# Attention steps in another order: both pairs' scores together, the quarters last

## The chip, the cores and the metric

The kernel runs on one core of one Trainium2 chip. The metric is device time in microseconds (us) of one execution; what is compared is the median of several. One execution of the kernel before was also recorded by the hardware profiler, and all traces shown are of that one.

The engines are named as the profile names them: PE is TensorE's products and PEld its loading of weights, DVE is VectorE, ACT is ScalarE, POOL is GpSimd, SP is SyncE, which issues every DMA of this kernel. Granted clock is the share of TensorE's full clock that the chip allowed.

## The reference

Sigmoid attention over 8 batches of 12 heads, 448 tokens, 64 numbers a head, then a dense layer with a squared ReLU:

```python
scores = scale * np.matmul(q, k.transpose(0, 1, 3, 2)) - np.log(S)
attn = 1.0 / (1.0 + np.exp(-scores))
attn_out = np.matmul(attn, v)
x = attn_out.transpose(0, 2, 1, 3).reshape(B * S, H * D)   # 3584 x 768
h = x @ w_in                                               # w_in is 768 x 2048
g = s * np.maximum(h, 0) ** 2 + b
out = g @ w_out                                            # 2048 x 768
```

All inputs of attention are float32; the two weight matrices arrive as float64 and are handed to the chip as pairs of words.

## The kernel before, in words

**Stages.** First attention, head by head, with its result written to DRAM as tokens (`x_dram`). Then, for the first 512 tokens, a plain dense layer (`ffn1`, `ffn2`) over 16 blocks of the hidden width. During this the weights are split in a rounded part and a rest and combined in sums, which are stored to DRAM (`wd`). Last, for two groups of three times 512 tokens, a fast scheme with fewer products reads these sums back as tiles `wu`; its first half writes `h`, its second half `o`.

**A quad.** Attention goes through 24 quads: four heads of one batch, as two pairs. The two heads of a pair lie on the two halves of the 128 partitions. For each pair `scores` makes three tiles `psc` of 128 keys by 448 queries, both heads side by side; a sigmoid on ScalarE (L347) turns each into a tile `a` in SBUF. The 448 keys are three blocks of 128 and a rest of 64. The rests of all four heads share one tile, `psc_l`, whose products use quarters of the array (`scores_last`, L368). `attn_v` (L378) multiplies `a` with v into `pav`, 64 columns a head, and `attn_v_last` (L387) adds the quarters. A product in float32 goes through TensorE in two passes, so each of these instructions stands twice in the profile. The score tiles rotate through three PSUM buffers, `pav0` and `pav1` have one each.

**A step.** The loop is pipelined over quads: step n makes the scores of quad n's first pair, attn @ v of both pairs of quad n-1, the scores of quad n's second pair and its quarters, and then the quarters of attn @ v of quad n-1. The result is copied from PSUM (`store_x`: the first pair by VectorE, the second by ScalarE) and stored.

**Weights beside attention.** A piece is a block of 128 rows or columns of one weight matrix: 768 float64 per partition, 768 KB. `piece` fetches it into a tile `st` and turns it into float32 with five VectorE instructions (L192 takes out the exponent; L198, L201, L205, L208) and one of ScalarE (L196) behind the first. All 32 pieces are done during attention, by a list that says how many belong to each step (`PIECES`). `sums_out` makes the sums of w_out and stores them. Which job comes in which part of a step is set by hand, with `at_step(n, when, fn)`; `ticks` runs the jobs of a part in the order of `when`.

**What sets the order.** Every engine runs its instructions in the order in which the program issues them. All DMAs go through SP, and its queue uses eight semaphores in turn (`DMAHW0` to `DMAHW7` in the program's waits), so a DMA is issued only after the eighth before it has landed. Slots of SBUF are handed out by hand (`Slots`); a tile in a reused slot waits for the earlier tile's last use.

**At the start** TensorE multiplies zeros (`idle`, six times) while the first loads run.

**At the change to the fast scheme** `load_raw` loads tokens (tiles `a_mk`, 512 KB each), `fetch` the tiles `wu` six ahead of use, and `out_store` writes the first outputs.

Of the kernel before, what the change touches and what calls it, by code (L numbers as in the profile page):

```python
# [11 lines left out]
F32 = mybir.dt.float32  # L12
# [71 lines left out]
def sigmoid_attention_relu2_ffn(  # L84
# [55 lines left out]

    heap = Slots(pool(ctx, "h0", 1), 1, "g")
    first = ExitStack()
    cx = Slots(pool(first, "cx", 1), 7, "c")
# [10 lines left out]
    nc.vector.memset(nls, -math.log(S))  # L154
    nc.scalar.activation(e_bias, nls, AF.Sigmoid)
    nc.vector.memset(e_bias, -896.0 * 2.0**23)
# [7 lines left out]
    def f32(ap):  # L164
        return ap.bitcast(F32)
# [4 lines left out]
    def sub(o, x, y):  # L170
        nc.vector.tensor_tensor(o, x, y, op=ALU.subtract)
# [100 lines left out]
    def sums_d(l, p, tl):  # L272

        _, x, sign, y = SUMS[l][3]
        t = tl.tile([P, 2, 2, KW], F32R, name=f"td_{l}_{p}")
        for j in range(2):
            op(f32(t[:, j, 1]), block(l, 2 * p + j, x), sign, block(l, 2 * p + j, y))
        yield
        nc.scalar.copy(t[:, :, 0], f32(t[:, :, 1]))
        yield  # L280
        sub(t[:, :, 1], f32(t[:, :, 1]), f32(t[:, :, 0]))
        nc.sync.dma_start(wd[l][p][:, 9], f32(t).rearrange("p j h c -> p j (h c)"))
        tl.free(t)
        yield
# [31 lines left out]


    at = ExitStack()
    ap_ = pool(at, "ap", 10)
    xo = pool(at, "xo", 3)  # L320
    ldv = pool(at, "ldv", 3)
    qk = ExitStack()
# [69 lines left out]
    def store_x(b, t, pavs):  # L392
        for i in range(2):
            o = xo.tile([P, S], F32, tag="xo", name=f"xo_{b}_{t}_{i}")
            if i:
                nc.scalar.copy(o, pavs[i][:, :S])
            else:
                nc.vector.tensor_copy(o, pavs[i][:, :S])  # L398
            nc.sync.dma_start(x_dram[b][:, 2 * t + i], o)

    loaded = {0: load(*quads[0], first=True)}

    zero = xo.tile([P, S], F32, tag="xo", name="zero").bitcast(BF16)
    nc.vector.memset(zero, 0.0)
    idle = ps_qk.tile([P, 2, 512], F32, tag="psc", name="idle")
    for _ in range(WARM):
        nc.tensor.matmul(idle[:, 0, :S], zero[:, :P], zero[:, :S], start=True, stop=True)

    plan = {}
    stores = []

    def at_step(n, when, fn):
        plan.setdefault((n, when > 5), []).append((when, len(plan.get((n, when > 5), ())), fn))

    def piece(l, f, n):
        st = []

        def fetch():
            st.append(cx.tile([P, DM], I64, name=f"st_{l}_{f}"))
            nc.sync.dma_start(st[0], (w_in, w_out)[l][f])

        at_step(n - 2, 5, fetch)
        g = []

        def last():
            next(g[0])
            cx.free(st[0])  # L430

        at_step(n - 1, 6, lambda: (g.append(convert(l, f, st[0])), next(g[0])))
        at_step(n - 1, 7, lambda: next(g[0]))
        at_step(n, 1, lambda: next(g[0]))
        at_step(n, 1, last)

    def sums_out(f, n):
        g = []
        at_step(n - 1, 8, lambda: (g.append(sums(1, f, cx)), next(g[0])))
        at_step(n, 2, lambda: next(g[0]))  # L440
        at_step(n, 9, lambda: next(g[0]))
        at_step(n + 1, 2, lambda: next(g[0]))
        at_step(n + 1, 9, lambda: next(g[0]))
        if f % 2:
            d = []
            at_step(n, 8, lambda: (d.append(sums_d(1, f // 2, heap)), next(d[0])))
            at_step(n + 1, 2, lambda: next(d[0]))
            at_step(n + 1, 9, lambda: next(d[0]))

    pieces = iter([(l, f + h * NP) for f in range(NP) for l in (1, 0) for h in range(2)])  # L450
    for n, m in enumerate(PIECES):
        for _ in range(m):
            piece(*next(pieces), n)
# [1 line left out]
    for f in range(NP):  # L455
        sums_out(f, SUMS_AT[f])

    def ticks(n, end=False):
        for _, _, fn in sorted(plan.pop((n, end), ()), key=lambda x: x[:2]):
            fn()  # L460

    loaded[1] = load(*quads[1])
    nc.sync.dma_start(s_sb, s)
    nc.sync.dma_start(b_sb, b_)
    ticks(-1)

    x0 = []
    blk = ExitStack()
# [14 lines left out]
        cx.free(w)  # L483
        return ph

    def first_tokens():
        for h in range(2):
            lo = cx.tile([P, HC, TB], F32R, name=f"x0l_{h}")
            load_tokens(f32(lo), 0, HC * h, HC)
            x0.append(lo)  # L490
        for h in range(2):
            yield
            lo = x0[h]
            hi = cx.tile([P, HC, TB], F32R, name=f"x0h_{h}")
            nc.scalar.copy(hi, f32(lo))
            sub(lo, f32(lo), f32(hi))
            x0[h] = (hi, lo)
        yield

    prev = None  # L500
    for n in range(NL + 1):
        cur = quads[n] if n < NL else None
        a, pavs = [], []
        if cur:
            a.append(scores(*cur, 0, loaded[n]))
        ticks(n)
        if n == NL - 2:
            ft = first_tokens()
            next(ft)
        if prev:  # L510
            for i in range(2):
                pavs.append(attn_v(*quads[n - 1], i, loaded[n - 1], prev[i]))
        if cur:
            a.append(scores(*cur, 1, loaded[n]))
            a.append(scores_last(*cur, loaded[n]))
        if prev:
            attn_v_last(loaded[n - 1], prev[2], pavs)
# [5 lines left out]
        if prev:  # L523
            store_x(*quads[n - 1], pavs)
        ticks(n, True)
        if n == NL - 1:
            qk.close()
            ps_h = pool(blk_ps, "ps_h", 2, space=PSUM)
            ps_av = pool(at, "ps_av2", 1, space=PSUM)
            next(ft)  # L530
            w1 = base(0, 0)
            next(ft)
        prev = a
    ph0 = ffn1(order[0], w1)
    at.close()

# [2 lines left out]
    p2 = pool(blk, "p2", 3)  # L539
    gp = pool(blk, "gp", 3)  # L540
    ps_o = pool(blk_ps, "ps_o", 1, space=PSUM)
    cx.more(pool(blk, "t2", 1), 5, "t")
    assert not plan

    threes = [tuple(1 + 3 * n + i for i in range(3)) for n in range((NT - 1) // 3)]
# [128 lines left out]
    for i, f in enumerate(order):  # L674
        ph = ffn1(f, w1) if i else ph0
        if i + 1 < NF:
            w1 = base(0, order[i + 1])
        if i == 0:
            w2[0] = base(1, order[0])
        for k in (k for k in range(NP) if 0 < i - sums_at[k] < 3):  # L680
            next(ts[k])
            next(ts[k])
        next(td, None)
        if i in sums_d_at:
            td = sums_d(0, sums_d_at.index(i), cx)
            next(td)
        if i and i in sums_at:
            next(ts[sums_at.index(i)])
        g = activate(f, ph)
        if i + 1 < NF:  # L690
            w2[i + 1] = base(1, order[i + 1])
        if i == 0:
            next(ts[0])
        if held:
            ffn2(*held, i == 1, False)
        held = (w2[i], g)
        if i == NF - 4:
            load_raw(0, *start[0])
            early.close()
            roll = pool(ctx, "roll", ROLL, side="right")  # L700
            heap.more(pool(ctx, "h1", 1, side="right"), 14, "r")
            for m, k in start[1:3]:
                load_raw(0, m, k)
            for _ in range(4):
                fetch()
        if i == NF - 3:
            for m, k in start[3:6]:
                load_raw(0, m, k)
            fetch()
        if i == NF - 2:  # L710
            for _ in range(5, AHEAD):
                fetch()
            for m, k in start[6:]:
                load_raw(0, m, k)
    for q_ in (4, 3):
        for fn in todo.pop(q_):
            fn()
# [17 lines left out]
    for o in outs:  # L735
        heap.free(o)
    ps = pool(ctx, "ps", 4, space=PSUM)

    def act_square(x):
# [24 lines left out]
    for n, blocks in enumerate(threes):  # L764
# [316 lines left out]
```

## Time and profile before

| | |
|---|---|
| time, median of 3 runs | 1069.99 us (1069.43 to 1070.44) |
| time of the profiled execution | 1071.2 us |
| its span, first to last instruction | 1069.4 us |
| mean granted clock | 0.998 |
| attention, to its last quarter | 0 to 277.65 us |
| plain dense layer | 277.65 to about 408 us |
| fast scheme | about 408 us to the end |
| HBM traffic | 262 GB/s over the span |

A row of a timeline gives start, length, engine, line, operation, what it writes and reads, the number of instructions merged in it, and in brackets how long the engine had stood idle before and what ended that. Rows of the chain that ended last give start, length and what the time went to. Groups give count, busy time, mean length in ns and idle time before them with its causes. A row of windows gives the stretch, its length, busy time of PE, PEld, DVE, ACT and POOL with the instructions touched, the granted clock, and the DMA engines' busy share and GB/s.

### The profile page before, as it was taken

Reading aid. Unit: us, or ns where it says so; the run is one execution under the profiler, and the core shown is the slowest. Engines: PE = TensorE matmul, PEld = TensorE weight load, DVE = VectorE, ACT = ScalarE, POOL = GpSimd, SP = SyncE. Lnnn points to the kernel's source line nnn. Section 1 sums busy time; section 2 is a strip of 40 time slices with the busy share of each in tenths; the row PEclk is TensorE's granted clock in tenths of the full one; section 3 lists DMA queues with packets and bytes.
Section 4 is the critical chain, followed back from the end, with each engine's and each line's share of the span. In section 5 each row is a group of like instructions: output and inputs, shape, how many; then the busy total and the mean of one; then the engine's idle time right before and its main releaser. Section 6 shows DMA issues by size and latency. Waiting matters only on the chain.

```text
span 1069.4 us, 13380 instructions
## 1 busy us (share of the span) xinstructions
PE 1059.4 (99%) x4998; PEld 753.7 (70%) x4998; DVE 780.7 (73%) x889; ACT 593.5 (55%) x662; POOL 0.2 (0%) x4
## 2 busy tenths in 40 slices
PE   8999999999999999999999999999999999999998
PEld 3333333333688887888888888888888888888886
DVE  3767766788787866365788889698545788888776
ACT  6878778778776656345336453343445336443432
POOL 0000000000000000000000000000000000000000
PEclk9999999999999999999999999999999999999999
DMA  7899888999898999766666677897666666676673
GB/s 288 274 351 361 315 319 331 364 334 335 310 394 321 371 359 405 234 194 196 196 192 189 194 233 227 263 325 270 197 194 196 195 190 191 194 230 220 213 229 109
DMA packets 105328, 280.86 MB, mean 263 GB/s; under 512 B 10544, under 2 KB 26416, under 8 KB 105264
## 3 DMA queue, kind: packets, MB, share of 16 engines
q1 hardware_dynamic: 105264, 280.01, 77.4%
q8 instruction: 40, 0.66, 0.2%
q14 instruction: 24, 0.20, 0.1%
HBM read 195.04 MB, written 84.93 MB: 262 GB/s over the span
## 4 chain that ended last, share of the span: by engine, by line
PE 94%; DMA 5%; ACT 0%; SPq 0%; DVE 0%; issue 0%; DVEq 0%; ACTq 0%
PE o L1024 31%; PE h L902 29%; PE psc L356 10%; PE pav L378 10%; PE ph L478 5%; PE po L659 5%; PE psc_l L368 2%; PE pav L387 2%; DMA wd<-w 1%; DMA st<-w_out 1%; DMA wu<-wd 1%; DMA a<-xd 1%; DMA wd<-t 1%; DMA q<-q_t 0%; SPq L311 0%
## 5 line engine op out<-in xcount | busy, mean ns | idle before, releaser
L347 ACT ACTIVATE a<-psc,nls 128x896 f32<-128x896 f32 x144 | 134.1, 1002 | 48.8 <-PE psc L356 48.7
L902 PE MATMUL h<-s_0h,wu 128*128 128x512 f32 x480 | 149.2, 392 | 1.8 <-DMA wu<-wd 1.8
L902 PE MATMUL h<-s_1h,wu 128*128 128x512 f32 x480 | 148.0, 389 | 0.0
L356 PE MATMUL psc<-q,k 64*128 64x448 f32 x576 | 122.8, 559 | 0.8 <-ACT a L347 0.8
L378 PE MATMUL pav<-a,v 128*64 128x448 f32 x576 | 113.5, 543 | 0.0
L902 PEld LDWEIGHTS h<-s_0h,wu 128*128 128x128 f32 x480 | 90.8, 189 | 21.1 <-ACT G L780 2.2
L902 PEld LDWEIGHTS h<-s_1h,wu 128*128 128x128 f32 x480 | 90.1, 188 | 18.8
L780 ACT COPY G<-h 128x1024 f32<-128x1024 f32 x48 | 48.8, 1017 | 96.8 <-PE h L902 68.1
L356 PEld LDWEIGHTS psc<-q,k 64*128 64x128 f32 x576 | 51.9, 188 | 71.0 <-issue 43.8
L747 ACT ACTIVATE G<-G,b_sb,s_sb 128x1024 f32<-128x1024 f32 x48 | 59.8, 1246 | 62.9 <-DVE G L744 62.2
L168 DVE TENSOR_TENSOR G<-G,h 128x1024 f32<-128x1024 f32 x40 | 48.8, 1219 | 62.2 <-PE h L902 62.2
L902 PE MATMUL h<-s_0l,wu 128*128 128x512 f32 x240 | 94.0, 391 | 0.0
L902 PE MATMUL h<-s_1l,wu 128*128 128x512 f32 x240 | 93.4, 389 | 0.0
L378 PEld LDWEIGHTS pav<-a,v 128*64 128x64 f32 x576 | 39.2, 137 | 71.4 <-issue 62.4
L1024 PE MATMUL o<-g_0h,wu 128*128 128x512 f32 x240 | 78.8, 389 | 0.0
L1024 PE MATMUL o<-g_1h,wu 128*128 128x512 f32 x240 | 78.8, 389 | 0.0
L1024 PE MATMUL o<-g_2h,wu 128*128 128x512 f32 x240 | 78.8, 389 | 0.0
L1024 PE MATMUL o<-g_3h,wu 128*128 128x512 f32 x240 | 78.8, 389 | 0.0
L659 PE MATMUL po<-g,w 128*128 128x512 f32 x288 | 67.7, 389 | 0.0
L659 PEld LDWEIGHTS po<-g,w 128*128 128x128 f32 x288 | 54.1, 188 | 11.2
L478 PE MATMUL ph<-x0h,w 128*128 128x512 f32 x192 | 61.7, 390 | 0.0
L398 DVE COPY xo<-pav 128x448 f32<-128x448 f32 x24 | 15.0, 624 | 60.5 <-PE pav L387 40.6
(127 smaller groups left out, 1831.2 us busy)
## 6 DMA issues: line engine op xcount, KB each, us to landing
wu<-wd SPq DMA_DIRECT2D x240, 512.0 KB, 3.5
wd<-t SPq DMA_DIRECT2D x48, 768.0 KB, 7.8
st<-w_out SPq DMA_DIRECT2D x16, 768.0 KB, 10.0
st<-w_in SPq DMA_DIRECT2D x16, 768.0 KB, 9.8
wd<-w SPq DMA_DIRECT2D x16, 768.0 KB, 4.3
v<-v_t SPq DMA_DIRECT2D x24, 448.0 KB, 7.2
xd<-xo SPq DMA_DIRECT2D x48, 224.0 KB, 8.8
k<-k_t SPq DMA_DIRECT2D x23, 448.0 KB, 4.5
```

What stands on the lines that cost most here:

```text
L168: nc.vector.tensor_tensor(o, x, y, op=ALU.add)
L347: nc.scalar.activation(a, psc[:, :, :S], AF.Sigmoid, bias=nls, scale=SCALE)
L356: nc.tensor.matmul(psc[:, j, :S], kt[r, i, c * P : (c + 1) * P], qt[r, i, :], start=True, stop=True,)
L368: nc.tensor.matmul(psc[half[i], j, :S], kt[r, i, 3 * P :], qt[r, i, :], start=True, stop=True,)
L378: nc.tensor.matmul(pav[r, :S], ld_[2][:, 3 * i + c, j, :], a[c][:, j, :], start=c == 0, stop=False,)
L387: nc.tensor.matmul(pavs[i][r, :S], ld_[2][half[i], 6, j, :], a[half[i], j, :], start=False, stop=True,)
L478: nc.tensor.matmul(ph, w[:, k, wi, kc * P : (kc + 1) * P], x0[h][xi][:, cc, :], start=m == 0, stop=m == 3 * NCC - 1,)
L659: nc.tensor.matmul(pos[e], w[:, k, wi, kc * P : (kc + 1) * P], g[:, gi, :], start=first and i == 0, stop=last and i == 2,)
L747: nc.scalar.activation(x, x, AF.Identity, bias=b_sb, scale=s_sb)
L780: nc.scalar.copy(g(m, h), bk)
L902: nc.tensor.matmul(bk[:, j], wt[:, j, wi, c * P : (c + 1) * P], opd[i][xi][:, c, :], start=i == ch[0] and m == 0, stop=m == 3 * KC - 1, sk ...
L1024: nc.tensor.matmul(bk[:, e], wt[:, f, wi, e * P : (e + 1) * P], g[gi][:, f, :], start=i == ch[0] and p == 0 and f == 0 and m == 0, stop=p ...
```

## The change

1. A step now belongs to one quad: scores of both pairs, attn @ v of both pairs, then the quarters of the scores of the *next* quad, and the quarters of attn @ v of this one. Only the quarters are still made a step ahead.
2. Jobs are placed by engine: those of a step's VectorE part stand ahead of its scores, those of its ScalarE part between scores and attn @ v, its DMAs behind the loads for quad n+2. A piece is fetched one step before its use instead of two. VectorE makes both result copies.
3. The piece list is shorter: the last two pieces of w_in are fetched and converted inside the plain dense layer (`LATE`). The first tokens are loaded two steps earlier, and the first block's split follows one step earlier.
4. At the start zeros are filled by VectorE's first instruction, in a tile of their own and half as long; nine idle products instead of six. The first two pieces are fetched ahead of the second quad.
5. At the change to the fast scheme four token tiles and three output stores move behind the first `wu` loads, to between later ones.

On TensorE, one step in the middle. `psc_1_0_0` is the first score tile of the first pair, `psc_2_l` the quarters of the next quad. Before:

```order
L356 MATMUL psc_1_0_2_239<-q_1_168,k_1_169 128x448 x2
L378 MATMUL pav_0_0_254<-a_0_0_0_183,v_0_153 64x448 x2
L378 MATMUL pav_0_1_261<-a_0_1_2_210,v_0_153 64x448 x2
L356 MATMUL psc_1_1_0_268<-q_1_168,k_1_169 128x448 x2
L356 MATMUL psc_1_1_2_278<-q_1_168,k_1_169 128x448 x2
L368 MATMUL psc_1_l<-q_1_168,k_1_169 64x448 x4
L387 MATMUL pav_0_0_254<-a_0_l,v_0_153 64x448 x2
L387 MATMUL pav_0_1_261<-a_0_l,v_0_153 64x448 x2
```

Now:

```order
L359 MATMUL psc_1_0_2_282<-q_1_175,k_1_176 128x448 x2
L359 MATMUL psc_1_1_0_287<-q_1_175,k_1_176 128x448 x2
L359 MATMUL psc_1_1_2_297<-q_1_175,k_1_176 128x448 x2
L381 MATMUL pav_1_0_311<-a_1_0_0_275,v_1_177 64x448 x2
L381 MATMUL pav_1_1_318<-a_1_1_2_300,v_1_177 64x448 x2
L371 MATMUL psc_2_l<-q_2_232,k_2_233 64x448 x4
L390 MATMUL pav_1_0_311<-a_1_l,v_1_177 64x448 x2
L390 MATMUL pav_1_1_318<-a_1_l,v_1_177 64x448 x2
```

The two blocks of scores of a step have become one, and attn @ v follows the scores of its own quad. (Rows between these continue their block.)

On SP, the start of the program (`k_0` and `q_0` belong to the first quad, `st` to pieces). Before:

```order
L342 DMA v_0_153<-v_t 128x896
L340 DMA k_1_169<-k_t 128x896
L341 DMA q_1_168<-q_t 128x896
L342 DMA v_1_170<-v_t 128x896
L463 DMA s_sb<-s_t 128x1
L464 DMA b_sb<-b_t 128x1
L423 DMA st_0_176<-w_out 128x768
L423 DMA st_8_178<-w_out 128x768
```

Now:

```order
L345 DMA v_0_155<-v_t 128x896
L425 DMA st_0_171<-w_out 128x768
L425 DMA st_8_173<-w_out 128x768
L343 DMA k_1_176<-k_t 128x896
L344 DMA q_1_175<-q_t 128x896
L345 DMA v_1_177<-v_t 128x896
L469 DMA s_sb<-s_t 128x1
L470 DMA b_sb<-b_t 128x1
```

The first two pieces have moved ahead of the second quad's loads.

On SP, the change to the fast scheme (`wu_0_4_3` and `wu_0_3_2` are its sixth and seventh weight tiles, `a_..` tokens, `o` outputs). Before:

```order
L557 DMA wu_0_4_3_3276<-wd_3_96 128x1024
L311 DMA a_11_3278<-xd_87 128x2x320
L311 DMA a_12_3281<-xd_87 128x2x320
L311 DMA a_10_3284<-xd_87 128x2x320
L246 DMA wd_3_96<-t_7_2_3236 128x3x512
L722 DMA out_t<-o_3372 128x2x512
L722 DMA out_t<-o_3380 128x2x512
L557 DMA wu_0_3_2_3390<-wd_2_95 128x1024
L557 DMA wu_0_3_3_3411<-wd_3_96 128x1024
```

Now:

```order
L560 DMA wu_0_4_3_3272<-wd_3_98 128x1024
L249 DMA wd_3_98<-t_7_2_3232 128x3x512
L560 DMA wu_0_3_2_3374<-wd_2_97 128x1024
L314 DMA a_01_3376<-xd_88 128x2x384
L560 DMA wu_0_3_3_3398<-wd_3_98 128x1024
L314 DMA a_11_3400<-xd_89 128x2x320
L560 DMA wu_0_10_0_3424<-wd_0_95 128x1024
L314 DMA a_12_3426<-xd_89 128x2x320
```

`wu_0_3_2` now follows the last store of sums; tokens and outputs come later, one between two `wu` loads. (A token tile is two issues where it spans two batches; one is shown.)

The diff, without renamed lines:

```diff
-WARM = 6
+WARM = 9
-PIECES = (0, 2, 1, 1, 2, 1, 1, 2, 1, 1, 2, 1, 1, 2, 1, 1, 2, 1, 1, 2, 2, 2, 1, 1)
+PIECES = (2, 1, 1, 2, 1, 1, 2, 1, 1, 2, 1, 1, 2, 1, 1, 2, 1, 1, 2, 1, 2, 1)
+LATE, LATE_AT, LATE_FOR = 2, 3, 4
...
+    zero = const.tile([P, S], BF16, name="zero")
+    nc.vector.memset(zero, 0.0)
...
-            if i:
-                nc.scalar.copy(o, pavs[i][:, :S])
-            else:
-                nc.vector.tensor_copy(o, pavs[i][:, :S])
+            nc.vector.tensor_copy(o, pavs[i][:, :S])
...
-        at_step(n - 2, 5, fetch)
+        at_step(n - 1, "SP", 0, fetch)
+        at_step(n, "DVE", 1, lambda: (g.append(convert(l, f, st[0])), next(g[0])))
+        at_step(n, "ACT", 1, lambda: next(g[0]))
+        if n:
+            at_step(n + 1, "DVE", 3, last)
+        else:
+            at_step(n, "ACT", 9, last)
...
+    for n, (b, t) in enumerate(quads):
+        ticks(n, "DVE")
+        a = [scores(b, t, i, loaded[n]) for i in range(2)]
+        if n == 0:
+            al = scores_last(b, t, loaded[0])
+        ticks(n, "ACT")
+        if n + 2 < NL:
+            loaded[n + 2] = load(*quads[n + 2])
+        ticks(n, "SP")
+        for fn in stores:
+            fn()
+        stores.clear()
...
+        pavs = [attn_v(b, t, i, loaded[n], a[i]) for i in range(2)]
+        last = al
+        if n + 1 < NL:
+            al = scores_last(*quads[n + 1], loaded[n + 1])
+        attn_v_last(loaded[n], last, pavs)
+        store_x(b, t, pavs)
...
+        j, stage = divmod(i - LATE_AT, LATE_FOR)
+        if 0 <= j < LATE:
+            if stage == 0:
+                st = cx.tile([P, DM], I64, name=f"st_{late[j][0]}_{late[j][1]}")
+                nc.sync.dma_start(st, w_in[late[j][1]])
+                cv = convert(*late[j], st)
+            elif stage < 4:
+                next(cv)
...
-            for m, k in start[3:6]:
+            for m, k in start[3:5]:
...
-        out_store(outs[-1], e, 0, 2)
...
+            if n == 0 and u < 4:
+                load_raw(0, *start[5 + u])
+            if outs and u > 4:
+                out_store(outs[0], evict[6 - 2 * len(outs)], 0, 2)
+                heap.free(outs.pop(0))
```

More of the change, by code (lines that the diff above doesn't have):

```diff
@@ L142, in sigmoid_attention_relu2_ffn @@
     first = ExitStack()
[L143 removed]
+    cx = Slots(pool(first, "cx", 1), 8, "c")
     wfp_last = pool(first, "wfp_last", 1)
@@ L394, in store_x, with at_step, ticks @@
             o = xo.tile([P, S], F32, tag="xo", name=f"xo_{b}_{t}_{i}")
-            if i:
-                nc.scalar.copy(o, pavs[i][:, :S])
-            else:
-                nc.vector.tensor_copy(o, pavs[i][:, :S])
+            nc.vector.tensor_copy(o, pavs[i][:, :S])
             nc.sync.dma_start(x_dram[b][:, 2 * t + i], o)
     loaded = {0: load(*quads[0], first=True)}
-    zero = xo.tile([P, S], F32, tag="xo", name="zero").bitcast(BF16)
-    nc.vector.memset(zero, 0.0)
     idle = ps_qk.tile([P, 2, 512], F32, tag="psc", name="idle")
     for _ in range(WARM):
-        nc.tensor.matmul(idle[:, 0, :S], zero[:, :P], zero[:, :S], start=True, stop=True)
+        nc.tensor.matmul(idle[:, 0, :S], zero[:, :P], zero, start=True, stop=True)
     plan = {}
     stores = []
-    def at_step(n, when, fn):
-        plan.setdefault((n, when > 5), []).append((when, len(plan.get((n, when > 5), ())), fn))
+    def at_step(n, part, rank, fn):
+        jobs = plan.setdefault((n, part), [])
+        jobs.append((rank, len(jobs), fn))
+    def ticks(n, part):
+        for _, _, fn in sorted(plan.pop((n, part), ()), key=lambda x: x[:2]):
+            fn()
     def piece(l, f, n):
@@ L429, in last @@
             next(g[0])
+            next(g[0])
             cx.free(st[0])
[L432 to L435, printed above, removed]
+        at_step(n - 1, "SP", 0, fetch)
[5 more added lines that the diff above has]
+            at_step(n, "ACT", 9, last)
     def sums_out(f, n):
         g = []
[L439 to L443, printed above, removed]
+        at_step(n, "DVE", 2, lambda: (g.append(sums(1, f, cx)), next(g[0])))
+        at_step(n, "ACT", 2, lambda: next(g[0]))
+        at_step(n + 1, "DVE", 2, lambda: next(g[0]))
+        at_step(n + 1, "ACT", 2, lambda: next(g[0]))
+        at_step(n + 2, "DVE", 2, lambda: next(g[0]))
         if f % 2:
             d = []
[L446 to L450, printed above, removed]
+            at_step(n + 1, "DVE", 2, lambda: (d.append(sums_d(1, f // 2, heap)), next(d[0])))
+            at_step(n + 1, "ACT", 3, lambda: next(d[0]))
+            at_step(n + 2, "DVE", 2, lambda: next(d[0]))
+    pieces = [(l, f + h * NP) for f in range(NP - 2) for l in (1, 0) for h in range(2)]
+    pieces += [(1, f + h * NP) for f in (NP - 2, NP - 1) for h in range(2)]
+    pieces += [(0, f + h * NP) for f in (NP - 2, NP - 1) for h in range(2)]
+    pieces, late = iter(pieces[:-LATE]), pieces[-LATE:]
     for n, m in enumerate(PIECES):
@@ L456, in sigmoid_attention_relu2_ffn @@
         sums_out(f, SUMS_AT[f])
-    def ticks(n, end=False):
-        for _, _, fn in sorted(plan.pop((n, end), ()), key=lambda x: x[:2]):
-            fn()
+    ticks(-1, "SP")
     loaded[1] = load(*quads[1])
@@ L484, in ffn1, with first_tokens, first_hi, first_lo @@
         return ph
[L486 to L517, printed above, removed]
+    def first_tokens(h):
+        lo = cx.tile([P, HC, TB], F32R, name=f"x0l_{h}")
+        load_tokens(f32(lo), 0, HC * h, HC)
+        x0.append(lo)
+    def first_hi(h):
+        hi = cx.tile([P, HC, TB], F32R, name=f"x0h_{h}")
+        nc.scalar.copy(hi, f32(x0[h]))
+        x0[h] = (hi, x0[h])
+    def first_lo(h):
+        hi, lo = x0[h]
+        sub(lo, f32(lo), f32(hi))
+    w1 = []
+    for h in range(2):
+        at_step(NL - 4, "SP", 1, lambda h=h: first_tokens(h))
+        at_step(NL - 2, "ACT", 7, lambda h=h: first_hi(h))
+        at_step(NL - 1, "DVE", 0, lambda h=h: first_lo(h))
+    at_step(NL - 2, "ACT", 8, lambda: w1.append(base(0, 0)))
+    for n, (b, t) in enumerate(quads):
[4 more added lines that the diff above has]
+        ticks(n, "ACT")
         if n + 2 < NL:
             loaded[n + 2] = load(*quads[n + 2])
+        ticks(n, "SP")
         for fn in stores:
@@ L528, in sigmoid_attention_relu2_ffn @@
             ps_h = pool(blk_ps, "ps_h", 2, space=PSUM)
[L529 to L533, printed above, removed]
+        pavs = [attn_v(b, t, i, loaded[n], a[i]) for i in range(2)]
[4 more added lines that the diff above has]
+        store_x(b, t, pavs)
+    ticks(NL, "DVE")
+    for fn in stores:
+        fn()
+    w1 = w1[0]
     ph0 = ffn1(order[0], w1)
@@ L691, in sigmoid_attention_relu2_ffn @@
             w2[i + 1] = base(1, order[i + 1])
+        j, stage = divmod(i - LATE_AT, LATE_FOR)
[6 more added lines that the diff above has]
+                next(cv)
+                if stage == 1:
+                    next(cv)
+                if stage == 3:
+                    cx.free(st)
         if i == 0:
```

12 lines of the change are left out of this document (2 added, 10 removed).

## The prediction

> **What bounds the kernel now.** I read the page's busy shares first, then who waited for whom on TensorE, then the chain of work that ended last.
>
> ```profile
> PE 1059.4 (99%) x4998; PEld 753.7 (70%) x4998; DVE 780.7 (73%) x889; ACT 593.5 (55%) x662; POOL 0.2 (0%) x4
> ...
> PE h L902 <- DMA wu<-wd: 1.8, 1, 1.8
> ```
>
> TensorE is busy all the time. Work taken off another engine is worth nothing; only shorter TensorE stretches count, and each new wait of TensorE counts in full. The chain shows what one step of attention is made of (start, length, engine, output tile, instructions):
>
> ```profile
> 24.87 2.46 PE psc L356 x12
> 27.32 4.66 PE pav L378 x24
> 31.98 2.46 PE psc L356 x12
> 34.44 0.91 PE psc_l L368 x8
> 35.35 0.75 PE pav L387 x8
> 36.10 2.46 PE psc L356 x12
> ...
> 272.07 4.66 PE pav L378 x24
> ...
> 277.65 8.41 PE ph L478 x36
> ```
>
> A step lasts 36.10 - 24.87 = 11.23 us, and 22 of them fill the 247.2 us to 272.07 (11.236 each), so no step has an irregular wait. The hole after the dense part is here, in the chain and in windows (length, busy time by engine, granted clock, DMA share, GB/s):
>
> ```profile
> 409.70 7.82 DMA a<-xd
> 417.54 8.91 DMA wu<-wd
> ...
> 426.59 148.75 PE h L902 x648
> ```
>
> ```profile
> 424.60:426.60 2.00, 0.18 (x2) 0.04 (x1) 0.38 (x1) 1.01 (x1) 0.00 (x0) 1.00 1.03 414
> 427.70:431.10 3.40, 3.40 (x10) 2.61 (x9) 0.00 (x0) 0.00 (x0) 0.00 (x0) 0.50 1.02 419
> ```
>
> TensorE stands for 1.8 us, and then 3.4 us pass at a granted clock of 0.50, which costs another 1.7. The late load was issued only at 417.54, when an older load landed (409.70 + 7.82); 8.91 us to landing with the DMA engines full did the rest.
>
> **The start.** These rows are of the timeline of the first 32 us, the last one of the DMA issues (count, KB, median us to landing).
>
> ```profile
> 0.80 0.06 DVE L154 MEMSET nls<- 128x1 f32 x1 [0.80 <-PEq L1071]
> ...
> 1.16 0.42 SPq L338 DMA_DIRECT2D q<-q_t  x1
> ...
> 2.39 0.43 DVE L404 MEMSET zero<- 128x448 uint32 x1
> ...
> 2.88 2.42 PE L407 MATMUL idle<-zero 128*128 128x448 bf16 x6 [2.88 <-DVE zero L404]
> ...
> 5.23 6.10 PE L356 MATMUL psc<-q,k 64*128 64x448 f32 x24
> ...
> 6.88 0.34 PEld L356 LDWEIGHTS psc<-q,k 64*128 64x128 f32 x2 [0.41 <-issue]
> ...
> 7.63 0.32 PEld L356 LDWEIGHTS psc<-q,k 64*128 64x128 f32 x2 [0.41 <-issue]
> ...
> 8.35 4.60 ACT L347 ACTIVATE a<-psc,nls 128x896 f32<-128x896 f32 x5 [0.20 <-PE psc L356]
> 8.52 0.19 PEld L356 LDWEIGHTS psc<-q,k 64*128 64x128 f32 x2 [0.19 <-issue]
> 8.89 0.19 PEld L356 LDWEIGHTS psc<-q,k 64*128 64x128 f32 x2 [0.19 <-issue]
> 9.41 0.42 PEld L356 LDWEIGHTS psc<-q,k 64*128 64x128 f32 x4 [0.33 <-ACT a L347]
> ...
> 12.18 2.75 PE L356 MATMUL psc<-q,k 64*128 64x448 f32 x12
> ...
> 16.04 0.56 DVE L192 TENSOR_SCALAR wf<-st 128x768 int32<-128x768 int32 x1 [13.22 <-DMA st<-w_out]
> ...
> 17.90 0.56 DVE L192 TENSOR_SCALAR wf<-st 128x768 int32<-128x768 int32 x1 [1.30 <-DMA st<-w_out]
> ...
> 18.38 0.98 DVE L198 SCALAR_TENSOR_TENSOR wf<-st,wf 128x768 int32<-128x768 int32 x1
> ...
> 21.86 0.95 DVE L198 SCALAR_TENSOR_TENSOR wf<-st,wf 128x768 int32<-128x768 int32 x1
> ```
>
> ```profile
> q<-q_t SPq DMA_DIRECT2D x2, 224.0 KB, 3.7
> ```
>
> *Idle products.* Zero is now filled by VectorE's first instruction, at 0.80 instead of 2.39, and is half as long: 0.2 us (0.43 at most). So the products begin at about 1.1. Six took 5.23 - 2.88 = 2.35 us to the first score, 0.39 each; nine take 3.5, and the first score comes at 4.6, 0.6 sooner. Its operands are there: the first q load was issued at 1.16 and is the quicker of two with a median of 3.7, so by 4.9 at worst.
>
> *Half clock.* One pass of scores took 0.74 us until 7.63 and 0.37 from 8.52 on. I read from this that the full rate came near 7.9, 5.0 after the first idle product, and that 2.7 us of scores ran at half rate, a loss of 1.3. With the same 5.0 the full rate comes at 6.1, and 1.5 us lose 0.75: a gain of 0.6. Bounds: full rate before the first score, a gain of 1.3; still only at 7.9, a loss of 0.3.
>
> The Trainium skill ("TensorE: Matmul & The Clock Gate", Part 1: The HAM clock gate) says that the full clock comes after one busy window of about 3.4 us that runs freely, which puts it 3.4 to 6.8 us after the first product; the trace's 5.0 lies inside. By its two ends the sum would be 1064.1 or 1065.7. The same section lets the clock fall only after an idle window as long; by it the hole above would be worth 1.8 and the sum 1066.5, but the rows show the half clock after 1.8 us of idling, and the measurement decides.
>
> *ScalarE.* Until 24.87 TensorE made 42 passes of 0.375 us (15.75) and, at full rate, some 1.07 us of switches between the forms of product (next part), 16.8 in all. It took 19.64 from 5.23. Of the 2.8 lost, 1.3 is the clock and 1.5 waits for ScalarE, since the software pipeline opened with eighteen passes of scores and nothing to put between. The new order puts attn @ v of the first step behind its own scores. The same 42 passes then cost 15.75 + 0.87 of switches + 0.75 of clock + two waits of 0.23 (below) = 17.8; begun at 4.6 they end at 22.4. **Term 1: -2.4 us.** Between the bounds of clock and fill: -1.3 to -3.1.
>
> *Loads at the start.* Two w_out pieces now stand in SP's queue ahead of the second quad's k, q and v. Pieces landed 1.86 us apart (16.04, 17.90), so that quad comes 3.7 later. It was there when its scores began at 12.18, hence by 15.9 now; its first use is the quarters behind the first step's attn @ v, after 26 passes (9.75), 0.67 of switches, a wait of 0.23 and the clock's 0.75 from 4.6, at 16.0. Cost nothing, though with little to spare by this bound; a later landing would be paid in full.
>
> **A step.** Passes follow each other by 0.375 us within a block (8.52 to 8.89). Six make 2.25 of the scores' 2.46, so a block of scores carries 0.2 of switching; twelve make 4.50 of the 4.66, so attn @ v carries 0.15; the quarters of scores carry 0.16 (0.75 of 0.91), the quarters of attn @ v behind them nothing. A step now has one block of scores instead of two: 0.2 saved. Whether the switch from attn @ v to quarters costs the 0.16 of the one from scores no row shows; a switch seen costs 0.15 to 0.2, and below nothing it cannot be, so 0.16 with a bound of 0.
>
> Against it stands a new wait: six score tiles follow one another on three PSUM buffers.
>
> ```profile
> 76.86 0.30 PEld L356 LDWEIGHTS psc<-q,k 64*128 64x128 f32 x4 [0.70 <-issue]
> 77.34 0.19 PEld L356 LDWEIGHTS psc<-q,k 64*128 64x128 f32 x2 [0.18 <-issue]
> ```
>
> ```profile
> 77.99 2.80 ACT L347 ACTIVATE a<-psc,nls 128x896 f32<-128x896 f32 x3 [2.13 <-PE psc L356]
> ```
>
> The first sigmoid starts 1.13 after the block, the next follow by 0.90, each lasts 1.0: buffers are free at 2.13, 3.03 and 3.93. TensorE, two passes a tile and 0.1 late at first (76.86 to 77.34 is 0.48), wants to begin the fourth tile at 2.35, the fifth at 3.10, the sixth at 3.85. From release to weights took 0.05 (8.35 + 1.01 to 9.41), from weights to product 0.1. So the fifth begins at 3.18 and the sixth at 4.08: 0.23 late, in every step. Bounds: nothing, if weights are loaded ahead; 6 x 0.90 - 4.7 = 0.7, if ScalarE sets the pace throughout. I take 0.23. **Term 2: 22 steps of -0.20 + 0.23, +0.7 us** (-7.9 to +11).
>
> The Trainium skill ("TensorEngine Tiling (Array Packing)", Key Properties) says that a change of tiling mode drains TensorE; the trace agrees, with 0.15 to 0.2 a switch, and by that alone a step would be 0.2 shorter. Its section PSUM Bottleneck speaks against the change: tiling quickens the products and not the emptying of PSUM; the trace agrees, 0.90 a tile against 0.75.
>
> Both result copies are VectorE's now, 0.62 each; ScalarE is rid of one.
>
> ```profile
> L398 DVE COPY xo<-pav 128x448 f32<-128x448 f32 x24 | 15.0, 624 | 60.5 <-PE pav L387 40.6
> ```
>
> They have the 4.9 us of the next scores before attn @ v needs the buffers: cost nothing.
>
> **The dense part after attention.** Both kernels run 32 blocks of the same products without a gap from 277.65. Two w_in pieces are now converted inside it instead of in attention. One piece costs VectorE four instructions behind the extraction and some 3.5 us (an estimate from 18.38 to 21.86, between the L198 of one piece and the next), spread over three pairs of blocks, 8.4 us each like the 36 products at 277.65, beside an engine that is 73% busy. Cost nothing; without that cover a late operand would stop TensorE by the overrun.
>
> At its end, the late load, wu_0_3_2, no longer stands behind a_01, a_11, a_12, a_10 (four tiles of 512 KB) and three outputs of as much: 3.7 MB at 414 GB/s, 8.9 us. The two pieces, 1.6 MB, may give 3.8 of that back, and TensorE comes 1.7 sooner. That leaves 3.4 against a lateness of 1.8. **Term 3: -1.8 - 1.7 = -3.5 us** (0 if a wait remains). The loads and stores taken away stand between later wu loads now; those are issued six tiles ahead, and 54 tiles of 12 products in 148.75 us are 2.75 each, so 16.5 us stand against the 8.91 that a landing took.
>
> **Sum.** -2.4 + 0.7 - 3.5 = -5.2. The profiled execution took 1071.2 with a span of 1069.4; its span should become 1064.2. The median shown is 1069.99, from which I subtract the same: **1064.8 us**.
>
> **Rivals.**
>
> *A: ScalarE keeps up.* The 0.23 does not appear, since weights may be loaded ahead: 1064.8 - 24 x 0.23 = 1059.3. This is also what the skill's drain rule alone would give. Against it: 9.41, where a weight load does wait for a sigmoid.
>
> *B: the hole stays.* Another load of the crowded queue is late and brings the same half clock: 1064.8 + 3.5 = 1068.3. For it: the DMA engines are at 1.02 to 1.03 there. Against: the 3.4 us above.
>
> *C: weight pieces land too late; slower.* They are now fetched one step ahead, behind the loads of k, q and v, which wait for the scores.
>
> ```profile
> 6.72 11.15 DMA st<-w_out
> ```
>
> ```profile
> L196 ACT ACTIVATE wf<-wf,e_bias 128x768 int32<-128x768 int32 x30 | 27.2, 932 | 2.0 <-DVE wf L192 0.3
> L239 ACT CAST t<-t 128x768 fp32r<-128x768 f32 x24 | 19.3, 842 | 0.0
> st<-w_out SPq DMA_DIRECT2D x16, 768.0 KB, 10.0
> ```
>
> Issued 4.95 + 3 x 0.42 = 6.2 into a step, landing 10.0 later is 5.0 into the next. VectorE works in order, ScalarE behind it: extraction (0.6), two L196 (1.9), a cast (0.8) and the quarters' sigmoid (0.9) must be done when the next step's first sigmoid is due, at 12.4. So a landing up to 8.2 hurts nothing, 13.2 us after the issue; the slow one above took 11.15. From there each us costs one in the seven steps that take two pieces: at 15 us, 7 x 1.8 = 12.6, or 1077. It decides from about 14 us.
>
> **How the numbers follow.** This kernel's measurement tells 0.2% (2.1 us) from no change, so faster means under 1067.85. My forecast has 0.68, A 0.12, B 0.12, C 0.08. The forecast's own range is 1062.5 to 1067 (term 1's bounds and 0.1 a step either way). Faster takes the forecast, A and a quarter of B: 0.83; same most of B: 0.09; slower C: 0.08. The range reaches to A and B and leaves out C and A's far half: 1060 to 1068.
>
> **What would show it.** Idle products from about 1.1, first score near 4.6, attention over near 275.9 (277.65). Steps of 11.26 with the scores' blocks at about 4.9, and the wait of psc weights on ACT a once a step. No wait of h on wu, and the clock at 1.00 around 425. I am wrong if steps come at 11.03 (A), if TensorE stands at the first h tiles (B), or if pav waits for copies or psc for sigmoids in every third step (C).

## The result and the profile after

The changed kernel takes **1081.8 us** (1080.33 to 1082.33) against 1069.89 of the kernel before on the same chip: a ratio of 1.0109, with a 95% interval of 1.0091 to 1.0126. It is 12 us slower, where 1064.8 was forecast and 1068 was the range's upper end. The profiled execution took 1082.22 with a span of 1080.1, 10.7 more than the span of before. One of the eight executions of the kernel with the rounded zero tile below had a mean granted clock of 0.753 and took 1335.38 us; without it that kernel's median of 1067.25 is 1067.05.

In the chain of waits of the changed kernel (start, length, what the time went to; L359 and L371 are the scores, L381 and L390 attn @ v, L483 and L662 the plain dense layer, L917 and L1039 the two halves of the fast scheme):

```profile
0.84 0.24 DVE zero L156
1.15 3.54 PE idle L405 x9
4.69 5.64 PE psc L359 x24
...
17.57 4.94 PE psc L359 x24
...
28.83 4.94 PE psc L359 x24
33.77 4.66 PE pav L381 x24
38.43 0.91 PE psc_l L371 x8
39.34 0.75 PE pav L390 x8
40.10 4.94 PE psc L359 x24
...
265.64 1.73 PE psc L359 x8
267.37 1.00 ACT a_l L350
268.42 3.71 PE psc L359 x16
...
277.71 8.40 PE ph L483 x36
...
340.76 8.96 DMA st<-w_in
...
364.18 4.08 PE ph L483 x18
...
425.84 150.36 PE h L917 x648
576.20 166.39 PE o L1039 x720
742.58 166.65 PE h L917 x720
909.23 166.38 PE o L1039 x720
```

Compare it stage by stage with the chain of before. The start and the steps are as forecast: the first idle product at 1.15, a step of 40.10 - 28.83 = 11.27, a block of scores of 4.94. But attention is over at 277.71, where it was over at 277.65. In the dense layer a late load stands in the chain, which was not there before. And the last rows are the surprise. Here are the same ones of the kernel before:

```profile
575.34 163.20 PE o L1024 x720
738.54 163.20 PE h L902 x720
901.74 163.21 PE o L1024 x720
```

The same 720 products take 166.4 to 166.7 us instead of 163.2: 231.1 to 231.5 ns from one to the next instead of 226.7, without a wait between them. The windows of the changed kernel (length, busy time of PE, PEld, DVE, ACT and POOL, granted clock, DMA share, GB/s) show nothing that would explain it:

```profile
427.70:431.10 3.40, 3.40 (x17) 2.81 (x16) 2.11 (x2) 1.02 (x1) 0.00 (x0) 1.00 1.05 391
440.00:480.00 40.00, 40.00 (x173) 32.16 (x172) 22.60 (x19) 16.58 (x17) 0.00 (x0) 1.00 0.62 211
```

Before, the second stretch read so:

```profile
440.00:480.00 40.00, 40.00 (x179) 33.10 (x178) 21.53 (x19) 17.96 (x18) 0.00 (x0) 1.00 0.66 194
```

Clock 1.00, TensorE busy throughout, much the same load on the DMA engines, and 173 products where there were 179. The first of the changed kernel's two rows shows no half clock at 428 to 431 us in this execution, as forecast. These are TensorE's waits in the changed kernel, without the one ahead of its first product:

```profile
...
PE psc L359 <- ACT a_l L350: 1.1, 1, 1.1
PE h L917 <- ACT G L790: 0.5, 1, 0.5
PE po L662 <- DVE g L174: 0.3, 1, 0.3
```

**Where 10.7 us of span come from.** From the starts of the first product of each stage: attention +0.06, dense layer +0.55, fast scheme to the end +10.08. The last is the sum of -3.64 for the hole and the half clock (661.13 us from the first `h` to the end before, 657.49 in the kernel with the rounded tile below), +0.6 for the wait on ACT G (the products on either side of it start 840 ns apart), and +13.1 for slower products: 2880 at a mean of 231.2 instead of 226.7.

### The profile page after: what moved, and what is told of

It reads as the page before. It is cut to its first block, busy times and chain, and to the rows that moved or that the text cites. A ratio compares the mean times of both kernels' runs of the same rounds, so it can differ in the third digit from the quotient of the medians.

```text
span 1080.1 us, 13352 instructions
## 1 busy us (share of the span) xinstructions
PE 1072.7 (99%) x5001; PEld 750.7 (70%) x5001; DVE 794.3 (74%) x913; ACT 584.0 (54%) x638; POOL 0.2 (0%) x4
## 4 chain that ended last, share of the span: by engine, by line
PE 93%; DVE 3%; DMA 2%; ACT 1%; issue 0%; SPq 0%; DVEq 0%
PE o L1039 31%; PE h L917 30%; PE psc L359 11%; PE pav L381 10%; PE ph L483 3%; PE po L662 3%; PE psc_l L371 2%; PE pav L390 2%; DMA st<-w_in 2%; DVE t L174 1%; DVE w L174 1%; DMA a<-xd 1%; DVE t L171 0%; PE idle L405 0%; DVE g L174 0%
## 5 line engine op out<-in xcount | busy, mean ns | idle before, releaser
L917 PE MATMUL h<-s_0h,wu 128*128 128x512 f32 x480 | 150.1, 393 | 0.5 <-ACT G L790 0.5
L917 PE MATMUL h<-s_1h,wu 128*128 128x512 f32 x480 | 150.1, 393 | 0.0
L350 ACT ACTIVATE a<-psc,nls 128x896 f32<-128x896 f32 x144 | 131.9, 1014 | 20.7 <-PE psc L359 20.7
L359 PE MATMUL psc<-q,k 64*128 64x448 f32 x576 | 121.7, 564 | 1.1 <-ACT a_l L350 1.1
L381 PE MATMUL pav<-a,v 128*64 128x448 f32 x576 | 113.5, 543 | 0.0
L917 PEld LDWEIGHTS h<-s_0h,wu 128*128 128x128 f32 x480 | 90.1, 188 | 21.7 <-ACT G L790 0.9
L917 PEld LDWEIGHTS h<-s_1h,wu 128*128 128x128 f32 x480 | 90.2, 188 | 21.1
L359 PEld LDWEIGHTS psc<-q,k 64*128 64x128 f32 x576 | 49.2, 187 | 73.2 <-ACT a L350 36.9
L917 PE MATMUL h<-s_0l,wu 128*128 128x512 f32 x240 | 94.3, 393 | 0.0
L917 PE MATMUL h<-s_1l,wu 128*128 128x512 f32 x240 | 94.3, 393 | 0.0
L381 PEld LDWEIGHTS pav<-a,v 128*64 128x64 f32 x576 | 39.2, 137 | 71.4 <-issue 48.4
L1039 PE MATMUL o<-g_3h,wu 128*128 128x512 f32 x240 | 79.9, 394 | 0.0
L1039 PE MATMUL o<-g_2h,wu 128*128 128x512 f32 x240 | 79.8, 393 | 0.0
L1039 PE MATMUL o<-g_0h,wu 128*128 128x512 f32 x240 | 79.8, 393 | 0.0
L1039 PE MATMUL o<-g_1h,wu 128*128 128x512 f32 x240 | 79.6, 393 | 0.0
L662 PE MATMUL po<-g,w 128*128 128x512 f32 x288 | 68.0, 389 | 0.3 <-DVE g L174 0.3
L195 DVE TENSOR_SCALAR wf<-st 128x768 int32<-128x768 int32 x32 | 18.0, 564 | 60.1 <-DMA st<-w_in 31.2
L662 PEld LDWEIGHTS po<-g,w 128*128 128x128 f32 x288 | 54.0, 188 | 11.8 <-DVE g L174 0.7
L483 PE MATMUL ph<-x0h,w 128*128 128x512 f32 x192 | 61.7, 390 | 0.0
```

Source lines behind the costliest of these rows:

```text
L350: nc.scalar.activation(a, psc[:, :, :S], AF.Sigmoid, bias=nls, scale=SCALE)
L359: nc.tensor.matmul(psc[:, j, :S], kt[r, i, c * P : (c + 1) * P], qt[r, i, :], start=True, stop=True,)
L381: nc.tensor.matmul(pav[r, :S], ld_[2][:, 3 * i + c, j, :], a[c][:, j, :], start=c == 0, stop=False,)
L483: nc.tensor.matmul(ph, w[:, k, wi, kc * P : (kc + 1) * P], x0[h][xi][:, cc, :], start=m == 0, stop=m == 3 * NCC - 1,)
L662: nc.tensor.matmul(pos[e], w[:, k, wi, kc * P : (kc + 1) * P], g[:, gi, :], start=first and i == 0, stop=last and i == 2,)
L917: nc.tensor.matmul(bk[:, j], wt[:, j, wi, c * P : (c + 1) * P], opd[i][xi][:, c, :], start=i == ch[0] and m == 0, stop=m == 3 * KC - 1, sk ...
```

## The experiments

**What was suspected.** The slow products begin in the fast scheme and nowhere else. Two things differ there from the rest: the order of loads and stores at its opening, and where its operands lie. The built program gives each tile its address within a partition. Tiles on the left side of SBUF are packed behind the constants. The new constant `zero`, 896 bytes, pushed them from 16640 (65 x 256) to 17536 (68.5 x 256). (The change also has one more slot in `cx` and two buffers fewer in `ap`, which the diff further up leaves out; they move tiles by whole multiples of 256 bytes.) The `wu` weights and 14 of the operand slots are packed from the right end and stayed at multiples of 256 (the lowest `wu` at 200448 = 783 x 256). So 2012 of the 2880 products now read a moving operand and weights whose starts differ by 128 modulo 256. In the dense layer both lie on the left and moved together, and its products kept 4.08 us for 18 (at 364.18 above; 4.08 before too).

Sorting the changed kernel's products by this difference: the 203 with equal starts whose three neighbours on either side are equal too follow each other by 227.8 ns, the 1131 unequal ones amid unequal ones by 232.8. What else reads and writes SBUF does not explain it: 134 of the 1131 ran while VectorE and ScalarE stood, 159 with less than one of the 16 DMA engines busy, and they follow each other by 232.7 and 232.5. That is a correlation; four runs put it to the test, against two rivals, the order of the queue and an unrecorded loss of clock.

### The zero tile rounded up

```diff
-    zero = const.tile([P, S], BF16, name="zero")
+    zero = const.tile([P, 512], BF16, name="zero")
```

(and the idle products read its first 448 columns).

> The zero tile is 1024 bytes per partition instead of 896, nothing else changes. Theory P (placement): the tile of 896 bytes moved everything that is allocated behind it on the left side of SBUF, so that the moving operands there begin 128 bytes past a multiple of 256 while the weights of the fast scheme, on the right side, still begin at a multiple of 256; with 1024 both agree again. P expects passes of 226.7 ns to the end, 653 us instead of 666.6 from the first h of the last stage to the end, and 1081.8 - 13.6 = 1068.2 us. Rival Q (order of the queue: later stores, other slots, loads between the weights) and rival C (the clock: without the half-clock stretch of before the chip runs slower afterwards, unrecorded) both expect passes of 227 to 238 ns as now and 1081.8 us.

Measured: 1067.25 us, ratio to before 0.9978 (0.9967 to 0.9988). Its chain:

```profile
408.20 163.20 PE h L917 x720
571.40 163.20 PE o L1039 x720
734.60 163.20 PE h L917 x720
897.80 163.21 PE o L1039 x720
```

One number in the tile's line, no instruction moved, and the span falls from 1080.1 to 1065.5 us: 13.1 of slow products, 0.6 of the wait on ACT G, which this profile doesn't show, and 0.9 in attention and the dense layer. The order of the queue is that of the changed kernel and there is no half clock here either, so both rivals fall.

### The kernel before, pushed

```diff
     e_bias = const.tile([P, 1], F32, name="e_bias")
+    gap = const.tile([P, 192], BF16, name="gap")
+    nc.vector.memset(gap[:, :1], 0.0)
```

> The kernel before with one more constant tile of 384 bytes per partition, of which one column is written and nothing is read: the left side of SBUF moves by 384 bytes, to 128 past a multiple of 256, all else stays. Theory P expects the fast scheme's passes to go from 226.7 to a mixture with a mean near 231, and the time from 1069.9 to about 1083. Rivals Q and C expect no change, 1069.9.

Measured: 1082.7 us, ratio 1.0121 (1.0106 to 1.0136). Its chain has the slow rows in the kernel before:

```profile
417.56 8.97 DMA wu<-wd
...
426.67 150.22 PE h L904 x648
576.89 166.20 PE o L1026 x720
743.09 166.88 PE h L904 x720
909.97 166.86 PE o L1026 x720
```

So the loss can be made without any part of the change.

### Both sides pushed

```diff
-    pool(ctx, "pad", 1, side="right").tile([P, 56], F32, tag="pad", name="pad")
+    pool(ctx, "pad", 1, side="right").tile([P, 88], F32, tag="pad", name="pad")
```

> The changed kernel with the pad on the right side of SBUF 128 bytes larger, so that weights and moving operands of the fast scheme all begin 128 past a multiple of 256. Theory P in its relative form (what counts is that weights and moving operand begin alike) expects 226.7 ns passes and 1068.2 us. P in its absolute form (a start off a multiple of 256 is slow by itself) expects all 2880 passes near 232.6 ns instead of two thirds of them, 1081.8 + 4 = 1086 us. Rivals Q and C expect 1081.8.

Measured: 1068.24 us, ratio 0.9985 (0.9976 to 0.9994).

```profile
571.89 163.20 PE o L1039 x720
735.09 163.20 PE h L917 x720
898.29 163.21 PE o L1039 x720
```

All starts are now off a multiple of 256 by 128, and all products are fast. What counts is that the two agree, not where they lie.

### The order of the queue alone

The kernel before with item 5 of the change and nothing else:

```diff
-            for m, k in start[3:6]:
+            for m, k in start[3:5]:
...
-            for m, k in start[6:]:
-                load_raw(0, m, k)
...
-        out_store(outs[-1], e, 0, 2)
...
-    for o in outs:
-        heap.free(o)
...
+            if n == 0 and u < 4:
+                load_raw(0, *start[5 + u])
+            if outs and u > 4:
+                out_store(outs[0], evict[6 - 2 * len(outs)], 0, 2)
+                heap.free(outs.pop(0))
```

> The kernel before with one part of the change alone: four token tiles are loaded, and three result tiles stored and freed, among the first products of the fast scheme instead of ahead of them. Term 3 of the prediction expects no wait of h on wu at 424 to 427 and no half clock behind it: 1069.9 - 3.5 = 1066.4 us. Theory P expects that with passes of 226.7 ns. Rivals Q and C, who hold this part of the change (or the half clock that it removes) responsible for the slow passes, expect 227 to 238 ns and 1066.4 + 13.6 = 1080 us.

Measured: 1067.31 us, ratio 0.9975 (0.9965 to 0.9985), with products of 226.7 ns and no wait of `h`. From the first `h` to the end it takes 657.44 us where the kernel before takes 661.13, 3.7 less, as term 3 said. The medians differ by 2.4 only. That fits a half clock that does not come behind the hole in every execution: of the 23 of the kernel before beside these four runs, four took 1071.2 to 1072.0 us, as the profiled one with its 1071.2, and the other nineteen 1068.0 to 1070.1. The mean granted clock does not settle it: the four list 0.998, but so do two of the nineteen. The pushed kernel has the hole too (TensorE waits 1.7 us for wu), and this is its window behind it, at full clock:

```profile
427.70:431.10 3.40, 3.40 (x17) 2.81 (x16) 0.00 (x0) 1.41 (x2) 0.00 (x0) 1.00 1.02 418
```

### How far apart

The changed kernel with the zero tile of 1024 bytes and 192 or 64 bytes more in the pad of the right side (104 or 72 floats instead of 56), and, last, with a zero tile of 1280 bytes.

> The changed kernel with the zero tile of 1024 bytes and 192 bytes more in the pad of the right side: the weights of the fast scheme begin 64 bytes past a multiple of 256, the moving operands of the left side at one; 2012 of 2880 passes are so mixed. Theory P, if any difference counts alike: passes with a mean near 231 ns and about 1080 us. If only a difference of 128 counts: 226.7 ns and 1067 us. If the cost grows with the difference: a mean near 229 ns and 1073.

> The same with 64 bytes more in the pad: the weights begin 192 past a multiple of 256, 64 below the moving operands. If any difference counts alike: a mean near 231 ns and about 1080 us. If only a difference of 128 counts: 226.7 ns and 1067 us. If the cost grows with the distance in either direction: as with 64 bytes; if with the difference taken one way: above the 231 ns of 128 bytes.

> The changed kernel with a zero tile of 1280 bytes: the moving operands of the left side begin 256 bytes apart from the weights, modulo 512. If the starts need to agree modulo 256, passes of 226.7 ns and 1067 us; if modulo 512, a mean near 231 ns and 1080 us.

Measured, one execution each: 1082.79, 1079.85 and 1068.15 us. The row of the second group's `h` in the chain with 192 bytes more:

```profile
741.59 167.49 PE h L917 x720
```

The same with 64 bytes more:

```profile
739.56 166.78 PE h L917 x720
```

And with the zero tile of 1280 bytes:

```profile
735.16 163.20 PE h L917 x720
```

| weights' start minus moving operand's, modulo 256 | mean distance of the fast scheme's products |
|---|---|
| 0 (before; both sides pushed; 256 apart) | 226.7 ns |
| 64 | 232.2 ns |
| 128 (the changed kernel; the pushed one) | 231.2, 231.4 ns |
| 192 | 231.1 ns |

(Waits and the half clock are left out of these means.) The three differences cost 4.4 to 5.5 ns a product, and the cost does not grow with the distance. A difference of 256 costs nothing. So of the differences tried, all multiples of 64, those that agree modulo 256 are free; smaller steps were not run.

### The start alone

The kernel before with nine idle products, and the zero tile filled ahead of the constants:

```diff
-WARM = 6
+WARM = 9
...
     nc.vector.memset(zero, 0.0)
+    nc.vector.memset(nls, -math.log(S))
+    nc.scalar.activation(e_bias, nls, AF.Sigmoid)
+    nc.vector.memset(e_bias, -896.0 * 2.0**23)
```

(the three lines that are added stood at the constants before).

> The kernel before with the start alone: the zero tile is filled first, and nine idle products are issued instead of six; the order of the steps stays. The prediction's first two parts of term 1 (0.6 of earlier start, 0.6 of clock) expect the first score at 4.6 and the first ph about 1.2 earlier than 277.58, and 1069.9 - 1.2 = 1068.7 us. The rival, that the first scores then wait for their loads or for ScalarE: nothing gained, 1069.9.

Measured: 1069.63 us, ratio 0.9999 (0.999 to 1.0008): nothing. The first score came at 4.48 instead of 5.23, but the first `ph` at 277.45 instead of 277.58. The waits say why:

```profile
PE psc L353 <- ACT a L344: 2.4, 2, 1.8
```

In the old order TensorE comes sooner to the place where it waits for ScalarE's sigmoids, and waits longer (0.8 before). The chain shows what that sigmoid itself stands behind:

```profile
7.62 10.14 DMA st<-w_out
...
18.38 0.94 ACT wf L193
...
19.31 0.91 ACT a L344
...
20.26 2.82 PE psc L353 x12
```

It stands behind the work on the second weight piece, and that piece lands at 17.76. In the kernel before it landed at 17.87 (6.72 + 11.15), and TensorE went on at 20.38. So the landing of a piece ends the opening there, however early the products begin. The changed kernel, which fetches the pieces ahead of the second quad and opens in another order, does not wait there. The 1.2 us that the prediction gave to earlier products and clock are not to be had by the start alone; which of these two other parts frees them, no run separates.

### Two attempts to mend the rest

The rows on ScalarE's timeline before the changed kernel's last step (start, length, then the instruction):

```profile
263.88 2.85 ACT L498 CAST x0h<-x0l 128x1536 fp32r<-128x1536 f32 x2
266.64 0.83 ACT L296 CAST w<-wf 128x768 fp32r<-128x768 f32 x1
267.37 1.00 ACT L350 ACTIVATE a_l<-psc_l,nls 128x896 f32<-128x896 f32 x1
```

The two `x0h` copies and the cast of `w` stand ahead of the quarters' sigmoid, which comes at 267.37. Two of the last step's six score tiles are done by then, and the third waits for the buffer of `psc_l`; by the chain above this block took from 265.64 to 268.42 + 3.71, 6.5 us instead of 4.94. The loss is not a fixed one: in the profiles of the five other kernels above that keep this order of instructions the block took 5.1 to 6.1. The first attempt, with the zero tile of 1024 bytes, moved one copy a step earlier, and the late pieces' loads ahead of the `w` stores of the same block:

```diff
-        at_step(NL - 2, "ACT", 7, lambda h=h: first_hi(h))
+        at_step(NL - 3 + h, "ACT", 7, lambda h=h: first_hi(h))
...
         g = activate(f, ph)
+        j, stage = divmod(i - LATE_AT, LATE_FOR)
+        if 0 <= j < LATE and stage == 0:
+            st = cx.tile([P, DM], I64, name=f"st_{late[j][0]}_{late[j][1]}")
+            nc.sync.dma_start(st, w_in[late[j][1]])
+            cv = convert(*late[j], st)
         if i + 1 < NF:
             w2[i + 1] = base(1, order[i + 1])
...
```

> The changed kernel with the zero tile of 1024 bytes and two further mends: one of the two x0h copies on ScalarE goes one step earlier, and the two late w_in pieces are fetched ahead of the w stores of their block. Theory P with the two small losses that the trace of the changed kernel shows (the last step's block of scores 6.49 us instead of 4.94, and 0.4 at the first late piece) expects attention over near 275.5, a dense part of 130.7, passes of 226.7 ns, and 1067.25 - 1.5 - 0.3 = 1065.4 us. If the last step's loss does not come from ScalarE's queue, attention stays over at 277.0 and the time at 1067.

Measured: 1067.37 us, no better than the rounded tile alone. The last block of scores is back at 4.94, but the one a step earlier now took 5.23, and attention was over only 0.5 sooner than with the rounded tile alone. The dense layer lost 0.9 instead of 0.3, at its second late piece and not at the first, which had been expected: the load, issued at 337.94, took 10.96 us, and VectorE, which works in order, stood before it with the following `g` behind it. Issued 1.7 us earlier, counted from the layer's start (337.94 - 276.51 against 340.76 - 277.64), a load that takes 9 to 11 still came late.

The second attempt put the second copy behind the last step's sigmoids and fetched each late piece a whole block of products (8.2 us) earlier:

```diff
-        at_step(NL - 2, "ACT", 7, lambda h=h: first_hi(h))
-        at_step(NL - 1, "DVE", 0, lambda h=h: first_lo(h))
+        at_step(NL - 2 + h, "ACT", 0 if h else 7, lambda h=h: first_hi(h))
+        at_step(NL - 1, "ACT" if h else "DVE", 4 if h else 0, lambda h=h: first_lo(h))
...
-            if stage == 0:
-                st = cx.tile([P, DM], I64, name=f"st_{late[j][0]}_{late[j][1]}")
-                nc.sync.dma_start(st, w_in[late[j][1]])
-                cv = convert(*late[j], st)
...
+        j, stage = divmod(i - LATE_AT + 1, LATE_FOR)
+        if 0 <= j < LATE and stage == 0:
+            st = cx.tile([P, DM], I64, name=f"st_{late[j][0]}_{late[j][1]}")
+            nc.sync.dma_start(st, w_in[late[j][1]])
+            cv = convert(*late[j], st)
```

> The changed kernel with the zero tile of 1024 bytes, the second x0h copy on ScalarE behind the last step's sigmoids instead of ahead of them, and the late w_in pieces fetched one block of 36 products earlier. If the 1.5 us of the last step come from ScalarE's queue and the stop at 358 us from a piece that takes 9 to 11 us to land, attention is over at 275.5, the dense part takes 130.7 and the time is 1067.25 - 1.5 - 0.3 = 1065.4 us. If both only move elsewhere, as in the mended kernel before this one, 1067.

Measured: **1066.1 us** (1065.62 to 1066.78), ratio 0.9965 (0.9953 to 0.9977), the fastest version run. Its chain:

```profile
265.51 4.94 PE psc L359 x24
270.45 4.66 PE pav L381 x24
275.11 0.91 PE pav L390 x8
276.02 8.40 PE ph L483 x36
...
406.82 163.20 PE h L917 x720
```

The last step is like all others, attention is over at 276.02, and from the first `ph` to the first `h` it takes 130.7 us, as the kernel before did.

## Why the prediction was wrong

**The step that failed.** The prediction ended its sum with the hole at 424 to 431 and took all work behind it as unchanged. Of `zero` it counted the filling (0.2 us) and the earlier products, not that a constant of 896 bytes pushes every tile allocated behind it. This term, +13.1 us, was missing altogether, and none of the rivals contained it: the only slower one (C, at 1077) was about landings. In these runs the change is slower for this reason alone; with the tile rounded up it is faster than before.

**Term 1 and term 2** (-2.4 and +0.7, attention over near 275.9). The first score came at 4.62 and the full clock at 6.19, forecast as 4.6 and 6.1. The 4.62 bears out the sum, the 6.19 is luck: in the seven other profiles with this start the full clock came anywhere from 4.73 to 6.99. The 42 passes that the prediction counted ended at 17.57 + 4.94 = 22.51, forecast as 22.4. The steps took 11.26 as forecast, and the new wait of score weights on sigmoids is in the waits of the changed kernel, 72 times in 24 steps, three a step where one was forecast:

```profile
PEld psc L359 <- ACT a L350: 36.9, 72, 0.7
```

With the last step mended attention ends at 276.02. So the sum of the two terms was right, but not in the kernel as it stands: the last step's 1.55 us ate nearly all of it. The prediction had added up ScalarE's jobs for the steps with pieces, not for the step in which the token copies land. Rival A, steps of 11.03, did not come. Inside term 1 the reading was wrong: the prediction put 1.5 us of waits down to an opening of eighteen passes of scores, but 0.8 of them ended with the sigmoid that stood behind a weight piece, and the run with the start alone shows that the first 1.2 us of the term are not gained as long as that wait stands. The sum came right all the same.

**The dense layer, "cost nothing".** It lost 0.55. The prediction weighed VectorE's work (3.5 us a piece) and not the wait of its in-order queue for a load of 9 us that is issued one block ahead.

**Term 3** (-3.5). Right for the profiled execution: 3.64 to 3.7. In the median it is worth 2.4, which fits a half clock that comes only in some executions. Taking the difference of a profile to be that of the median is the mis-sized part: the mended version has the span forecast (1064.1 for 1064.2) and a median 1.3 above the forecast of 1064.8. Rival B, another late load, came in a small form and without the half clock, the 0.6 on ACT G. It was a store and not a load: the profile has ScalarE stand 4.5 us, until 421.05, for a store of sums (`wd`), and its copies of `h` come late behind that. With both sides pushed it stood 4.6 and TensorE waited again; with the rounded tile alone it stood 3.0 and TensorE did not. So this is no fixed cost.

**Rival C.** No step of attention waits for weight pieces.

## What to carry to other kernels

A new constant is not free because it is small: it moves everything allocated behind it. Before an edit that adds or resizes a tile is costed, look up where the two operands of the hot products start, and in a stream like this one round the tile up so that they keep agreeing modulo 256 bytes; afterwards compare the time of an equal count of products in the chain of both kernels, since a pass that is 2% longer shows in no list of waits and in no clock. When work is moved between steps, add up the in-order queue of each engine for the very step that receives it, loads that it must wait for included.

## What was not expected of the hardware

**Products slow down by 2% when the starts of weights and moving operand differ modulo 256 bytes.** The Trainium skill ("SBUF — State Buffer", Who interferes with whom) says that TensorE reads the moving operand and the weights through two independent ports and never waits on anyone; these runs show that the two reads are not wholly independent, with 226.7 ns against 231.1 to 232.2. The same page (Operand start alignment) states what starts are legal and says that it times nothing. All of this is shown for float32r products of 512 columns that stream one behind the other, with 2012 of 2880 products unequal (2020 in the pushed kernel). Whether bfloat16 or the float32 products of attention do the same no run shows, since their starts agreed in every kernel here, and by what mechanism the two reads meet stays open.

**The half clock behind a short hole is not certain.** TensorE's wait for wu was followed by 3.4 us at half clock in the kernel before (1.8 us) and in the start alone (1.9), and by none in the pushed kernel (1.7). Whether the length decides or the moment, no run shows.

**The full clock comes at no fixed time after the first product.** From the first idle product it took 5.0 us in the kernel before (2.88 to 7.88), 5.0 in the changed one (1.15 to 6.19), 3.2 in the pushed one (2.88 to 6.05) and 2.7 in the start alone (1.38 to 4.03). The Trainium skill ("TensorE: Matmul & The Clock Gate", Part 1: The HAM clock gate) explains a spread of 500 ns to either side by a window that runs freely; the spread here is wider, and the shortest of these are below the one whole window of about 3.4 us that it asks for.
